# A linear attention fused with a gated feed-forward block: another table of orders, engines, PSUM banks and load places

## The chip, the cores and the metric

The kernel runs on one core of one Trainium2 chip. The metric is the device time of one execution in microseconds, lower is better; the number compared is the median over several executions. The core has five engines with an instruction queue each: PE (matmul), DVE (elementwise), ACT (activations and copies), POOL (elementwise, and the issue of DMAs whose descriptors are made by software) and SP (here only DMA issues). An instruction waits in its engine's queue until what it reads is there and what it overwrites is no longer needed, and nothing behind it on that engine starts before it.

## What is computed

Inputs r, k, v, w have the shape (batch 4, heads 8, time 768, 48), u is (8, 48), and the four weights are w1 and w2 (384 x 1024), w3 (1024 x 1024) and w_out (1024 x 384), all float32. The output is 3072 x 384.

```python
def _attn_ref(r, k, v, w, u):
    state = zeros(B, H, D, D)
    for t in range(S):
        kt, vt, rt, wt = (k[:, :, t], v[:, :, t], r[:, :, t], w[:, :, t])
        cur = einsum('bhd,bhe->bhde', u[None] * kt, vt)
        y[:, :, t] = einsum('bhd,bhde->bhe', rt, state + cur)
        state = wt[:, :, :, None] * state + einsum('bhd,bhe->bhde', kt, vt)
    return y

def _moe_ref(x, w1, w2, w3, w_out):
    a = x @ w1
    b = x @ w2
    h = a * b @ w3
    return h @ w_out
```

x is y with the heads side by side, one row for each time step of each batch element.

## The kernel before

Time is cut into 6 chunks of 128 steps, and the work into 13 units, numbered 0 to 12: units 0, 1 and 2 are chunk 0 of batch element 0, of 1, and of 2 and 3; from unit 3 on each unit is one chunk of two batch elements. A unit's steps carry its number.

Within a unit the recurrence becomes matmuls over a chunk: ln (L408, ACT) takes the logarithm of w; cs (L424, PE) sums it up along time, csT (L453) does so transposed; ne, e and et (ACT) are the exponentials of these sums; KRk, KRr and KRw (DVE or POOL) scale k and r with them; trk, trr and trw (PE) transpose, trke and trre copy the transposed tiles out of PSUM. From unit 7 or 8 on, DMA transposes on SP (dtr, dtk) do this work. m (L551, PE) multiplies the scaled k and r; its result is masked to the past either by one DVE product (msk, L570), or by a copy on ACT (mcp, L557) and a mask on POOL or DVE (maff). yi (L596) and ys (L586) sum up the output on PE, from within the chunk and from the state. rk, ruk, dg and dv form the part with u, yb (L614, DVE) adds it, yt and xT (or the DMA transposes dty) make the transposed x. kv, T, S and Sb carry the state to the next chunk.

For the feed-forward block, w3 @ w_out is formed once: for each of 8 row blocks, wt (L371) transposes a block of w3, w3Te copies it out, wm (L380) multiplies it by w_out, w34e copies the product to w34. Then, for each unit and each group g of columns, a (L714) and b (L714) multiply x by w1 and w2, asb (L719, ACT) copies a out, abT (L724, DVE) multiplies it by b; o (L730) multiplies by w34, osb (L735) copies out, st (L740, SP) stores. Units 0 and 1 have half the columns of the others. The last of w3's transposes free the tile w3_bf, whose space then takes r and k of later units; wo_bf does so for v. `warm` is a run of matmuls of zeros, that touch no data.

Loads: w, k, r and v of each unit (win, kin, rin, vin) and the weights in pieces (w1, w2 in two halves, w3 in four quarters, w_out as one). Unit 0 has r, k, v and u loaded on SP as float32 and cast by rc, kc, vc, uc; all other loads of the opening are issued by POOL.

Nothing orders the work at run time but the engines' queues. The order is one written list, `ORDER`: each entry is a step and the engine that it goes to, and the kernel records the steps in that order, so that each engine's queue is the list cut down to its own entries. `BANKS` gives every step its PSUM banks (eight) and, for copies, its buffer number; a bank must be emptied by the copy of its last user before a matmul may write it. `POOL_MASK` names the m blocks that are masked by mcp and maff.

```python
for e in ORDER.split():
    name, _, eng = e.partition("@")
    if name.startswith("warm"):
        warm(int(name[4:]), int(eng))
        continue
    steps[name](eng)
```

Of the kernel before, what the change touches and what calls it, by code (L numbers as in the profile page):

```python
# [40 lines left out]
tk0=0 m0_0=4,5 M0_0=0 y0=3,4 yt0=6 kv0=6 a0_0=6 b0_0=6 sa0_0=2 a0_1=2 b0_1=0 sa0_1=0 o0_0=0 so0_0=0 cs1=7 ct1=2 tr1=0
tk1=4 m1_0=4,5 M1_0=3 y1=3,4 yt1=1 kv1=3 a1_0=1 b1_0=0 sa1_0=0 a1_1=5 b1_1=2 sa1_1=2 o1_0=1 so1_0=1 cs2=2,3 ct2=0,1
tr2=2 tk2=7 m2_0=5,6 M2_0=2 m2_1=2,3 M2_1=1 y2=4,5 yt2=1 kv2=7 a2_0=5 b2_0=4 sa2_0=1 a2_1=7 b2_1=7 sa2_1=0 a2_2=1
b2_2=4 sa2_2=0 a2_3=0 b2_3=1 sa2_3=1 o2_0=5 so2_0=3 o2_1=2 so2_1=2 cs3=5,6 ct3=5,6 tr3=4 tk3=2 m3_0=3,4 M3_0=2
m3_1=5,6 M3_1=0 y3=0,1 yt3=6 kv3=1 a3_0=5 b3_0=4 sa3_0=2 a3_1=5 b3_1=3 sa3_1=2 a3_2=2 b3_2=3 sa3_2=1 a3_3=5 b3_3=2
sa3_3=0 o3_0=2 so3_0=3 o3_1=5 so3_1=2 cs4=3,4 tr4=6 tk4=3 m4_0=4,5 M4_0=3 m4_1=2,3 M4_1=1 y4=6,7 yt4=6 kv4=4 a4_0=7
b4_0=3 sa4_0=0 a4_1=3 b4_1=4 sa4_1=0 a4_2=5 b4_2=2 sa4_2=1 a4_3=4 b4_3=6 sa4_3=2 o4_0=3 so4_0=2 o4_1=0 so4_1=3 cs5=0,1
tr5=0 tk5=4 m5_0=0,1 M5_0=3 m5_1=0,1 M5_1=2 y5=6,7 yt5=3 kv5=7 a5_0=1 b5_0=2 sa5_0=1 a5_1=4 b5_1=3 sa5_1=0 a5_2=0
b5_2=6 sa5_2=1 a5_3=5 b5_3=6 sa5_3=2 o5_0=4 so5_0=1 o5_1=3 so5_1=0 cs6=0,1 ct6=0,1 tr6=1 tk6=7 m6_0=2,3 M6_0=1
m6_1=2,3 M6_1=0 y6=0,1 yt6=7 kv6=4 a6_0=1 b6_0=0 sa6_0=2 a6_1=2 b6_1=5 sa6_1=2 a6_2=0 b6_2=7 sa6_2=1 a6_3=2 b6_3=4  # L50
sa6_3=0 o6_0=2 so6_0=1 o6_1=6 so6_1=3 cs7=6,7 tk7=0 m7_0=1,2 M7_0=2 m7_1=4,5 M7_1=3 y7=0,1 yt7=1 kv7=7 a7_0=3 b7_0=7
sa7_0=1 a7_1=4 b7_1=2 sa7_1=1 a7_2=3 b7_2=7 sa7_2=0 a7_3=6 b7_3=4 sa7_3=2 o7_0=2 so7_0=2 o7_1=4 so7_1=0 cs8=1,2
m8_0=5,6 M8_0=0 m8_1=2,3 M8_1=1 y8=0,1 kv8=6 a8_0=5 b8_0=6 sa8_0=0 a8_1=3 b8_1=3 sa8_1=1 a8_2=6 b8_2=5 sa8_2=0 a8_3=7
b8_3=5 sa8_3=2 o8_0=7 so8_0=1 o8_1=2 so8_1=1 cs9=4,5 m9_0=4,5 M9_0=3 m9_1=0,1 M9_1=2 y9=0,1 kv9=7 a9_0=0 b9_0=3
sa9_0=1 a9_1=1 b9_1=6 sa9_1=0 a9_2=4 b9_2=7 sa9_2=2 a9_3=4 b9_3=2 sa9_3=2 o9_0=7 so9_0=2 o9_1=6 so9_1=0 cs10=5,6
m10_0=2,3 M10_0=0 m10_1=0,1 M10_1=1 y10=6,7 kv10=4,5 a10_0=4 b10_0=3 sa10_0=2 a10_1=4 b10_1=5 sa10_1=2 a10_2=4 b10_2=5
sa10_2=1 a10_3=2 b10_3=2 sa10_3=0 o10_0=3 so10_0=3 o10_1=5 so10_1=2 cs11=0,1 m11_0=4,5 M11_0=2 m11_1=6,7 M11_1=3
y11=0,1 a11_0=2 b11_0=4 sa11_0=1 a11_1=1 b11_1=7 sa11_1=0 a11_2=6 b11_2=4 sa11_2=0 a11_3=0 b11_3=6 sa11_3=2 o11_0=7
so11_0=0 o11_1=2 so11_1=0 cs12=0,1 m12_0=2,3 M12_0=1 m12_1=4,5 M12_1=0 y12=0,1 a12_0=2 b12_0=1 sa12_0=0 a12_1=7
# [6 lines left out]
m_0_0@PE w3_0@POOL u@SP uc@ACT mask@POOL rin_1@POOL vin_0@SP vc_0@ACT kv_0@PE ruk_0@DVE dg_0@DVE dv_0@POOL csT_2@PE
ne_2@ACT KRk_2@DVE trk_2@PE trw_2@PE S_0@DVE msk_0_0@DVE yi_0_0@PE kin_1@POOL rk_2@DVE et_2@ACT trke_2@ACT w1_1@POOL
ruk_2@POOL KRw_2@DVE yb_0@DVE warm5@3 m_2_0@PE m_2_1@PE mcp_2_1@ACT ln_1@ACT msk_2_0@DVE warm4@6 cs_1@PE yi_2_0@PE
dg_2@DVE csT_1@PE pc_1@ACT ne_1@ACT wt_0_0@PE wt_0_1@PE maff_2_1@DVE yt_0@PE xT_0@ACT yi_2_1@PE pc_2@ACT kv_2@PE
et_1@ACT dv_2@DVE KRk_1@DVE wt_1_0@PE trw_1@PE wt_1_1@PE yb_2@DVE yt_2@PE a_0_1@PE KRw_1@DVE trk_1@PE xT_2@ACT  # L70
trke_1@ACT a_2_3@PE S_2@DVE m_1_0@PE w3Te_1@ACT a_2_2@PE w1_0@POOL a_0_0@PE a_2_1@PE w2_1@POOL asb_2_2@ACT vin_1@POOL
b_2_3@PE w3Te_0@DVE msk_1_0@DVE rk_1@POOL yi_1_0@PE a_2_0@PE ruk_1@DVE dg_1@DVE dv_1@DVE Sb_2@DVE asb_2_3@ACT
abT_2_3@DVE yb_1@DVE b_0_1@PE yt_1@PE xT_1@DVE asb_0_0@ACT asb_2_0@ACT kv_1@PE b_2_2@PE abT_2_2@DVE a_1_0@PE
asb_0_1@ACT abT_0_1@DVE w2_0@POOL b_0_0@PE a_1_1@PE b_2_0@PE asb_2_1@ACT S_1@DVE b_1_1@PE wo@POOL abT_0_0@DVE wm_1@PE
asb_1_1@ACT b_2_1@PE w34e_1@DVE abT_2_1@DVE win_3@POOL ln_3@ACT wm_0@PE cs_3@PE ne_3@ACT b_1_0@PE w3_1@POOL wt_2_0@PE
wt_2_1@PE csT_3@PE asb_1_0@ACT abT_1_1@DVE Sb_0@DVE wt_3_0@PE abT_2_0@DVE kin_3@POOL KRk_3@DVE wt_3_1@PE w3Te_2@DVE
rin_3@POOL trk_3@PE rk_3@DVE trw_3@PE w34e_0@ACT wm_2@PE pc_3@ACT et_3@ACT KRw_3@DVE trke_3@ACT m_3_1@PE w34e_2@DVE
m_3_0@PE w3_2@POOL wt_4_0@PE wt_4_1@PE win_4@POOL w3Te_3@ACT wm_3@PE wt_5_0@PE wt_5_1@PE msk_3_1@DVE mcp_3_0@ACT
maff_3_0@DVE w3Te_4@ACT wm_4@PE abT_1_0@DVE w3_3@POOL w34e_3@DVE ln_4@ACT Sb_1@ACT iw_4@ACT vin_3@POOL w3Te_5@DVE
cs_4@PE ruk_3@DVE e_4@ACT dg_3@DVE w34e_4@DVE ys_3@PE ne_4@ACT wt_6_0@PE wt_6_1@PE w3Te_6@DVE wm_5@PE wt_7_0@PE  # L80
wt_7_1@PE yi_3_0@PE yi_3_1@PE dv_3@DVE yb_3@DVE win_5@POOL ln_5@ACT w3Te_7@DVE rin_4@POOL rw_4@DVE wm_6@PE w34e_6@ACT
cs_5@PE pc_5@ACT yt_3@PE xT_3@DVE ne_5@ACT pc_4@ACT wm_7@PE a_3_1@PE KRr_4@DVE trr_4@PE e_5@ACT kin_4@POOL KRk_4@DVE
trk_4@PE rk_4@DVE kv_3@PE w34e_7@DVE vin_4@POOL kv_4@PE trre_4@DVE iw_5@ACT asb_3_1@ACT w34e_5@ACT o_0_0@PE T_4@DVE
ruk_4@DVE rin_5@POOL trke_4@ACT m_4_1@PE T_3@DVE m_4_0@PE ys_4@PE rw_5@DVE msk_4_1@DVE osb_0_0@ACT win_6@POOL ln_6@ACT
dg_4@DVE o_1_0@PE osb_1_0@ACT o_2_1@PE osb_2_1@ACT st_2_1@SP cs_6@PE ne_6@ACT b_3_1@PE msk_4_0@DVE kin_5@POOL
# [704 lines left out]
```

## Time and profile before

| | us |
|---|---|
| median of 3 executions | 168.65 |
| lowest and highest of them | 168.05 and 200.98 |
| the profiled execution | 168.6 |
| its span, from the first to the last instruction | 166.9 |

The profile is one execution of the program taken by the hardware profiler. Its busy times are shares of the span; matmuls are pipelined and their ends modelled, so that a busy PE isn't PE at its peak. What a stage costs is read from the wait that ends last in it: the timeline names, in brackets, the idle time before an instruction and what ended it. Idle time of an engine that isn't the bound costs nothing. The names there are those of tiles: lw is written by ln, NEt by ne, ETt by et, KR by KRk and KRr, KRT by the transposed copies, Mbf by msk, mcp and maff, w_bf stands for all weight tiles, banks is PSUM.

### The profile page before, as it was taken

What the parts mean: (1) busy time and instruction counts of PE and PEld (TensorE: products, weight loads), DVE (VectorE), ACT (ScalarE), POOL (GpSimd) and SP (SyncE); (2) the same over time, 40 slices, a digit from 0 to 9 for tenths busy, and PEclk for the clock granted to TensorE, in tenths of its full rate; (3) what the DMA queues carried; (4) which work ended last, traced back from release to release, by engine and by line L of the source; (5) the groups of instructions that cost most, each with busy time, mean ns of one, the idle gap of its engine ahead of it and who ended that gap; (6) DMA issues with size and microseconds to landing.
All of it is one profiled execution on the core that took longest, in us unless ns stands there. A gap on an engine that the chain in (4) does not pass through costs nothing.

```text
span 166.9 us, 4592 instructions
## 1 busy us (share of the span) xinstructions
PE 154.8 (93%) x1912; PEld 118.1 (71%) x1913; DVE 129.7 (78%) x203; ACT 96.9 (58%) x160; POOL 106.7 (64%) x96
## 2 busy tenths in 40 slices
...
GB/s 113 215 163 180 163 188 195 245 168 245 207 151 180 141 65 235 144 157 240 108 180 195 147 207 157 84 96 172 187 137 97 108 164 164 20 166 116 4 113 125
DMA packets 100789, 25.63 MB, mean 154 GB/s; under 512 B 92928, under 2 KB 98688, under 8 KB 100768
## 3 DMA queue, kind: packets, MB, share of 16 engines
...
q14 instruction: 6, 0.05, 0.1%
...
## 4 chain that ended last, share of the span: by engine, by line
PE 74%; DVE 13%; DMA 5%; issue 4%; ACT 3%; POOL 1%; DVEq 0%; ACTq 0%; POOLq 0%
PE banks L714 31%; PE banks L730 16%; PE banks L380 6%; DMA win<-in_w_dram 5%; PE banks L551 4%; DVE Mbf L570 3%; PE banks L596 2%; PE banks L371 2%; PE banks L512 2%; DVE dv L539 2%; PE banks L424 2%; DVE KR L445 2%; PE banks L667 2%; PE banks L633 1%; DVE yb L614 1%
## 5 line engine op out<-in xcount | busy, mean ns | idle before, releaser
L714 PE MATMUL banks<-xT,w_bf 128*128 128x256 bf16 (+1 forms) x624 | 69.6, 264 | 1.7 <-DVE Mbf L570 1.7
L714 PEld LDWEIGHTS <-w_bf 128*128 128x128 bf16 x624 | 55.7, 98 | 9.4 <-issue 2.1
L719 ACT COPY a_sb<-banks 128x512 f32<-128x512 f32 x48 | 27.3, 590 | 25.8 <-PE banks L714 14.0
L724 DVE TENSOR_TENSOR abT<-a_sb,banks 128x512 bf16<-128x512 f32 x48 | 31.8, 681 | 8.6 <-PE banks L714 5.7
L730 PE MATMUL banks<-w,abT 128*128 128x384 bf16 x192 | 34.2, 326 | 0.0
L730 PEld LDWEIGHTS <-abT 128*128 128x128 bf16 x192 | 18.1, 98 | 10.7
L570 DVE TENSOR_TENSOR Mbf<-banks,mask 128x1024 bf16<-128x1024 f32 x14 | 17.1, 1218 | 4.3 <-PE banks L551 4.3
L735 ACT COPY osb<-banks 128x384 f32<-128x384 f32 x19 | 9.0, 480 | 14.1 <-PE banks L730 13.1
L614 DVE TENSOR_TENSOR yb<-banks,dv 128x768 bf16<-128x768 f32 (+1 forms) x13 | 11.6, 890 | 4.4 <-POOL dv L539 2.4
L335 POOL DMA_DIRECT2D win<-in_w_dram x12 | 13.9, 1158 | 1.4 <-POOLq L774 0.8
L408 ACT ACTIVATE lw<-win 128x768 bf16<-128x768 f32 (+1 forms) x13 | 10.4, 802 | 6.9 <-DMA win<-in_w_dram 6.9
L557 ACT CAST Mbf<-banks 128x1024 bf16<-128x1024 f32 x10 | 10.2, 1016 | 5.2 <-PE banks L551 3.7
L441 ACT ACTIVATE NEt<-banks 128x768 bf16<-128x768 f32 (+1 forms) x13 | 9.9, 761 | 4.2 <-PE banks L424 2.5
L565 POOL TENSOR_SCALAR_AFFINE_SELECT Mbf<-Mbf 128x1024 bf16<-128x1024 bf16 x5 | 5.4, 1102 | 10.5 <-ACT Mbf L557 10.5
L380 PE MATMUL banks<-wo_bf,w3T 128*128 128x384 bf16 x64 | 11.7, 326 | 0.0
L530 DVE TENSOR_REDUCE dg<-ruk 128x16 f32<-128x768 bf16 (+1 forms) x13 | 11.5, 885 | 0.1
L335 POOL DMA_DIRECT2D vin<-in_v_dram x8 | 9.1, 1140 | 3.8 <-DMA wo_bf<-in_moe_w_out_dram 3.2
L335 POOL DMA_DIRECT2D kin<-in_k_dram x8 | 9.1, 1142 | 3.0 <-PE banks L380 2.7
L335 POOL DMA_DIRECT2D rin<-in_r_dram x8 | 9.0, 1128 | 2.9 <-DMA w_bf<-in_moe_w_dram 2.2
L308 PE MATMUL banks<-zeros 128*128 128x512 bf16 x26 | 9.5, 525 | 1.5 <-DVE zeros L249 1.3
L486 POOL TENSOR_TENSOR KR<-rw,Et 128x768 bf16<-128x768 bf16 x3 | 4.9, 1639 | 8.5 <-DVE rw L478 5.4
L424 PE MATMUL banks<-lw,LT 128*128 128x384 bf16 x24 | 6.2, 325 | 2.7 <-ACT lw L408 1.8
(102 smaller groups left out, 257.2 us busy)
## 6 DMA issues: line engine op xcount, KB each, us to landing
out_dram<-osb SPq DMA_DIRECT2D x24, 192.0 KB, 2.3
...
w_bf<-in_moe_w_dram POOLq DMA_DIRECT2D x4, 512.0 KB, 13.3
...
kin<-in_k_dram POOLq DMA_DIRECT2D x7, 192.0 KB, 9.3
rin<-in_r_dram POOLq DMA_DIRECT2D x7, 192.0 KB, 9.5
vin<-in_v_dram POOLq DMA_DIRECT2D x7, 192.0 KB, 7.5
wo_bf<-in_moe_w_out_dram POOLq DMA_DIRECT2D x1, 768.0 KB, 10.6
```

Of the source, the lines that this page charges most:

```text
L335: QUEUE[eng].dma_start(dst, src)
L380: nc.tensor.matmul(one(f"wm{fi}")[:, :DM], lhsT=w3T[fi % 2][:, gi, :], rhs=wo_bf[:, gi, :], start=(gi == 0), stop=(gi == FI - 1))
L408: nc.scalar.activation(LW[:, :, :D], ww, Act.Ln)
L441: nc.scalar.activation(N_.rearrange("t (b h) d -> t b (h d)", b=nb), cs_view(), Act.Exp, scale=-1.0)
L530: nc.vector.reduce_sum(dgs, ruks, axis=AX.X)
L557: copier(eng)(Mbf[bank[f"M{t}_{b}"]], mview())
L570: nc.vector.tensor_mul(Mbf[bank[f"M{t}_{b}"]], mview(), mask.rearrange("s (j q) t -> s j q t", j=2))
L614: nc.vector.tensor_add(ybs.rearrange("t b (q e d) -> t e (b q) d", e=2, d=D), yview().rearrange("t e (x d) -> t e x d", d=D), dvs.rearrang ...
L714: nc.tensor.matmul(o[:, f, :], lhsT=wt[:, di, fi * P:(fi + 1) * P], rhs=x[:, di, :T], start=(di == 0), stop=(di == DI - 1))
L719: copier(eng)(a_sb[bank[f"sa{t}_{g}"]], one(f"a{t}_{g}"))
L724: nc.vector.tensor_mul(ab[:, g * per:(g + 1) * per, :T], sa.rearrange("p (f t) -> p f t", t=T), one(f"b{t}_{g}").rearrange("p (f t) -> p f ...
L730: nc.tensor.matmul(one(f"o{t}_{b}")[:, :DM], lhsT=ab[:, fi, b * C:(b + 1) * C], rhs=w34[:, fi, :], start=(fi == 0), stop=(fi == FI - 1))
```

## The change

Three tables are replaced: `POOL_MASK`, `BANKS` and `ORDER`. Functions, shapes, buffers and the arithmetic stay as they are. Every step is there before and after; the matmuls of zeros were 27, in runs of 13, 5, 3 and 6, and are 32, in runs of 17, 2, 3, 3, 4 and 3.

```diff
-POOL_MASK = {(2, 1), (3, 0), (5, 1), (6, 1), (7, 1), (8, 0), (8, 1), (10, 0), (11, 1), (12, 1)}
+POOL_MASK = {(2, 1), (5, 1), (6, 1), (7, 1), (8, 1), (9, 1), (10, 0), (11, 0), (12, 0)}
...
-wt0=3 wm0=3 wt1=6 wm1=0 wt2=7 wm2=7 wt3=1 wm3=1 wt4=2 wm4=5 wt5=7 wm5=7 wt6=6 wm6=5 wt7=2 wm7=2 cs0=0 ct0=1 tr0=7
+wt0=7 wm0=3 wt1=6 wm1=6 wt2=2 wm2=2 wt3=7 wm3=4 wt4=3 wm4=2 wt5=7 wm5=7 wt6=4 wm6=4 wt7=3 wm7=3 cs0=5 ct0=0 tr0=3
...
-table@ACT zeros@DVE padkr@DVE padet@DVE padlw@DVE win_0@POOL ln_0@ACT padr@DVE ones@DVE win_2@POOL kin_2@POOL LT@POOL
+table@ACT zeros@DVE vin_0@SP win_0@POOL kin_0@SP ones@DVE win_2@POOL kin_2@POOL rin_2@POOL padet@DVE I128@POOL u@SP
```

Steps that change their engine: osb of 1_0, 2_1, 3_1, 4_1, 5_0, 8_1 and 9_0 from ACT to DVE, of 5_1 and 10_0 from DVE to ACT; KRk of 0, 7, 9 and 11 from POOL to DVE, of 1 and 12 from DVE to POOL; S of 3, 4 and 7 to POOL, of 9 and 10 to DVE; dv of 6 and 10 to POOL, of 7 and 11 to DVE; rk of 8 and 11 to POOL, of 1 and 9 to DVE; ruk of 1 to POOL, of 2 and 9 to DVE; rw of 10 to POOL; maff of 2_1 and 7_1 from DVE to POOL; rc_0 from DVE to ACT and vc_0 from ACT to DVE; Sb, trke, xT, w3Te and w34e each in two to four cases; win_9 from SP's queue to POOL's.

The end of the list: before, the order on PE behind the last b was b_12_1, o_11_1, o_10_1, o_12_1, o_12_0, o_11_0; now it is b_12_1, o_11_1, o_11_0, o_12_0, o_12_1.

Three places in the engines' queues follow. In these rows a number behind a tile's name is its buffer, and a last number its place among all tiles.

First, ACT at the program's start, from ln_0 on, as one piece of the difference. win_0 is unit 0's w, win_2 unit 2's, win_1 unit 1's.

```order
 L408 ACTIVATE lw_0_82<-win_0_78 128x8x48
 L441 ACTIVATE NEt_0_90<-banks_61 128x384
+L330 CAST rin_0_62<-wide_r0_156 128x8x48
+L304 CAST u_bc_153<-u_f_154 128x384
 L459 ACTIVATE ETt_0_92<-banks_61 128x4x128
 L408 ACTIVATE lw_0_82<-win_2_80 128x16x48
-L436 ACTIVATE pc_0_112<-banks_61 128x4
-L304 CAST u_bc_153<-u_f_154 128x384
-L330 CAST vin_0_72<-wide_v0_157 128x384
 L441 ACTIVATE NEt_0_90<-banks_61 128x768
 L459 ACTIVATE ETt_0_92<-banks_61 128x8x128
+L436 ACTIVATE pc_0_112<-banks_61 128x4
```

The casts of r and u now stand ahead of et_0 and of unit 2's ln; the cast of v has left ACT. On SP, the four loads of unit 0 went out in the order r, k, u, v and now do in the order v, k, u, r.

Second, POOL in the opening, from w1's first half on; before:

```order
L346 DMA w1_bf_141<-in_moe_w1_dram 128x3x512
L524 TENSOR_TENSOR ruk_0_104<-rk_0_102,u_bc_153 128x768
L346 DMA w1_bf_141<-in_moe_w1_dram 128x3x512
L350 DMA w2_bf_142<-in_moe_w2_dram 128x3x512
L335 DMA vin_1_73<-in_v_dram 128x8x48
L520 TENSOR_TENSOR rk_1_103<-rin_1_63,kin_1_68 128x384
L350 DMA w2_bf_142<-in_moe_w2_dram 128x3x512
L354 DMA wo_bf_144<-in_moe_w_out_dram 128x8x384
L335 DMA win_3_81<-in_w_dram 128x16x48
L361 DMA w3_bf_143<-in_moe_w3_dram 128x2x1024
```

and now:

```order
L346 DMA w1_bf_141<-in_moe_w1_dram 128x3x512 x2
L350 DMA w2_bf_142<-in_moe_w2_dram 128x3x512
L445 TENSOR_TENSOR KR_1_95<-kin_1_68,NEt_1_91 128x8x48
L565 AFFINE_SELECT Mbf_2_100<-Mbf_2_100 128x1024
L335 DMA vin_1_73<-in_v_dram 128x8x48
L350 DMA w2_bf_142<-in_moe_w2_dram 128x3x512
L354 DMA wo_bf_144<-in_moe_w_out_dram 128x8x384
L524 TENSOR_TENSOR ruk_1_105<-rk_1_103,u_bc_153 128x384
L335 DMA win_3_81<-in_w_dram 128x16x48
L361 DMA w3_bf_143<-in_moe_w3_dram 128x2x1024
```

Both halves of w1 and the first of w2 now go out with no product between them; KRk_1, the mask of 2_1 and ruk_1 have come to POOL, ruk_2 and rk_1 have left it, and win_3 stands behind ruk_1.

Third, DVE around the m block of unit 9, before (msk_9_1, T_9, KRk_10 and msk_9_0 are the second to the fifth row):

```order
L724 TENSOR_TENSOR abT_7_136<-a_sb_1_127,banks_61 128x512
L570 TENSOR_TENSOR Mbf_2_100<-banks_61,mask_149 128x1024
L674 TENSOR_TENSOR Tst_0_116<-banks_61,Sst_0_118 128x384
L445 TENSOR_TENSOR KR_0_94<-w3_bf_143,NEt_0_90 128x16x48
L570 TENSOR_TENSOR Mbf_3_101<-banks_61,mask_149 128x1024
L724 TENSOR_TENSOR abT_7_136<-a_sb_0_126,banks_61 128x512
```

and now (rk_9, an abT, KRk_10, msk_9_0, ruk_9 and dg_9):

```order
L520 TENSOR_TENSOR rk_1_103<-w3_bf_143 128x768
L724 TENSOR_TENSOR abT_7_136<-a_sb_2_128,banks_61 128x512
L445 TENSOR_TENSOR KR_0_94<-w3_bf_143,NEt_0_90 128x16x48
L570 TENSOR_TENSOR Mbf_0_98<-banks_61,mask_149 128x1024
L524 TENSOR_TENSOR ruk_1_105<-rk_1_103,u_bc_153 128x768
L530 TENSOR_REDUCE dg_1_107<-ruk_1_105 128x16
```

Block 1 of unit 9 is no longer masked there (it goes by ACT and POOL), T_9 has moved to later, rk_9 and ruk_9 have come from POOL, and msk_9_0 still follows KRk_10.

172 lines of the change are left out of this document (86 added, 86 removed).

## The prediction

> **What bounds the kernel now.** I read the page's busy times first, then PE by stages, then the chain of waits, then the opening instruction by instruction. Lines of the page: busy time, share of the span, instructions.
>
> ```profile
> PE 154.8 (93%) x1912; PEld 118.1 (71%) x1913; DVE 129.7 (78%) x203; ACT 96.9 (58%) x160; POOL 106.7 (64%) x96
> ```
>
> The same by stages: in each row the stretch, its length, then busy time of PE, PEld, DVE, ACT, POOL.
>
> ```profile
> 20.00:36.00 16.00, 14.79 (x225) 13.02 (x221) 12.01 (x21) 8.14 (x16) 12.11 (x13) 1.00 1.41 201
> 36.00:60.00 24.00, 24.00 (x330) 17.83 (x328) 21.25 (x36) 17.13 (x28) 12.18 (x11) 1.00 1.95 176
> 60.00:84.00 24.00, 23.28 (x347) 18.84 (x345) 22.87 (x32) 18.44 (x31) 22.10 (x19) 1.00 1.96 165
> 84.00:96.00 12.00, 11.45 (x143) 9.10 (x141) 11.17 (x19) 9.30 (x15) 9.32 (x7) 1.00 1.71 176
> 96.00:115.00 19.00, 17.89 (x240) 13.75 (x238) 18.49 (x24) 13.64 (x23) 15.96 (x12) 1.00 1.31 140
> 115.00:164.00 49.00, 48.18 (x533) 37.62 (x530) 31.26 (x47) 21.55 (x38) 17.62 (x14) 1.00 0.72 122
> ```
>
> From 36 us on PE is the bound: its idle time there is 0, 0.72, 0.55 and 1.11 us, and after 115 nothing until its last matmul. So a new order has three places to gain: the opening up to 36 us, 2.4 us of idle PE in the middle, and the tail. DVE is a close second: from 36 to 115 us it is busy 73.8 of 79 us, so 5.2 us are free. The chain of waits, in order of time, gives the joints:
>
> ```profile
> 23.39 0.51 PE banks L633 x6
> ...
> 34.91 1.30 PE banks L380 x8
> ...
> 47.66 0.55 PE banks L371 x8
> ...
> 143.59 5.90 PE banks L714 x54
> ...
> 156.68 6.51 PE banks L730 x40
> 163.26 0.48 ACT osb L735
> ```
>
> 23.39 is yt_2, the transpose that lets unit 2 into the wide matmuls; 34.91 is wm_1, the first product of w3 and w_out; 163.26 is the last copy. 54 matmuls in 5.90 us make 0.109 us each for 256 columns, 8 transposes in 0.45 to 0.55 us some 0.056 each.
>
> **The opening, step by step.** These are timeline rows of before: start, duration, what.
>
> ```profile
> 1.25 5.73 PE L308 MATMUL banks<-zeros 128*128 128x512 bf16 x13 [1.25 <-DVE zeros L249]
> 2.77 0.43 SPq L326 DMA_DIRECT2D wide_v<-in_v_dram  x1
> 7.50 0.32 PE L424 MATMUL banks<-lw,LT 128*128 128x384 bf16 x1 [0.52 <-ACT lw L408]
> 8.25 0.59 ACT L459 ACTIVATE ETt<-banks 128x512 bf16<-128x512 f32 x1
> 10.33 0.84 ACT L408 ACTIVATE lw<-win 128x768 bf16<-128x768 f32 x1 [1.49 <-DMA win<-in_w_dram]
> 11.14 0.50 ACT L304 CAST u_bc<-u_f 128x384 bf16<-128x384 f32 x1
> 11.23 0.48 PE L424 MATMUL banks<-lw,LT 128*128 128x384 bf16 x2 [1.31 <-ACT lw L408]
> 11.54 0.51 ACT L330 CAST vin<-wide_v 128x384 bf16<-128x384 f32 x1
> 11.95 0.81 ACT L441 ACTIVATE NEt<-banks 128x768 bf16<-128x768 f32 x1
> 12.79 1.22 DVE L445 TENSOR_TENSOR KR<-kin,NEt 128x768 bf16<-128x768 bf16 x1 [0.18 <-ACT NEt L441]
> 13.00 1.02 ACT L459 ACTIVATE ETt<-banks 128x1024 bf16<-128x1024 f32 x1 [0.24 <-PE banks L453]
> 15.14 1.01 ACT L516 COPY KRT<-banks 128x1024 bf16<-128x1024 bf16 x1 [1.12 <-PE banks L512]
> 17.49 0.62 PE L551 MATMUL banks<-KRT 64*128 64x128 bf16 x16
> 17.93 1.23 DVE L570 TENSOR_TENSOR Mbf<-banks,mask 128x1024 bf16<-128x1024 f32 x1 [0.70 <-PE banks L551]
> 19.07 0.94 DVE L530 TENSOR_REDUCE dg<-ruk 128x16 f32<-128x768 bf16 x1
> 19.93 0.68 DVE L563 TENSOR_TENSOR Mbf<-Mbf,mask 128x1024 bf16<-128x1024 bf16 x1
> 20.52 1.67 DVE L539 TENSOR_TENSOR dv<-vin,dg 128x768 bf16<-128x768 bf16 x1
> 22.39 0.94 DVE L614 TENSOR_TENSOR yb<-banks,dv 128x768 bf16<-128x768 f32 x1
> 23.05 1.17 POOL L335 DMA_DIRECT2D win<-in_w_dram  x1
> ```
>
> And issue to landing (last figure, us) of SP's fourth load, and of the last w3 load, issued at 29.07:
>
> ```profile
> wide_v<-in_v_dram SPq DMA_DIRECT2D x1, 192.0 KB, 7.2
> ...
> w_bf<-in_moe_w_dram POOLq DMA_DIRECT2D x1, 512.0 KB, 16.1
> ```
>
> SP's queue. r of unit 0 changes places with v: it was the first load there; as fourth it lands where v did, 2.77 + 7.2 = 9.97. ACT now has rc_0 and uc ahead of et_0 and ln_2, so they queue behind that landing: rc_0 9.97 to 10.48 (0.51, the equal cast of v), uc to 10.98, et_0 to 11.57, ln_2 to 12.41. cs_2 thus starts near 12.45, where it was 11.23: 1.2 us lost. Four more matmuls of zeros put cs_0 at 7.9 to 8.6 for 7.50 (13 took 5.73, 0.44 each; at full clock half); that costs nothing, since et_0 waits for 10.98 anyway. If r came early, it would cost up to 1.1.
>
> What makes it up. ACT: ne_2 from 12.9 to 13.7, et_2 to 14.8, pc_0, ln_1 (half of 0.84, and a start) and pc_2 to 15.6. DVE: msk_0_0 ends at 13.9 (1.23 after dg_0), KRk_2 at 14.5 or 15.1 (half of, or all of, the 1.22 seen beside POOL's dv_0). trke_2 then ends at 16.6 to 17.3, m_2_1 follows, and msk_2_0 starts at 17.6 to 18.4, behind yb_0, rk_2, S_0 and ruk_2 on DVE: before 17.93. Behind it DVE has lost maff_2_1 (0.68), which goes to POOL: dg_2 ends 2.15 after msk_2_0's start, dv_2 takes 0.95 (like dg_2) to 1.67, yb_2 0.94. yt_2 so starts between 21.7 and 23.3, and was at 23.39. I take the middle, 22.5, as neither end of the two unknown contentions is nearer: 0.9 us won, bounds 0.1 and 1.7.
>
> From yt_2 to wm_1 before took 11.52 us. In it lie 126 matmuls of L714, 42 with 256 columns (4.6 us) and 84 with 128 (half of 0.109 each, 4.6), and 13 transposes, m_1_0, yi_1_0 and kv_1 with 1.4: 10.6 in all, so 0.9 is waiting. Now trk_1 (0.2) is done ahead of yt_2, where PE waits, and b_0_1 (0.65) stands between yi_1_0 and yt_1, which cover the wait for yb_1. I take 0.2 + 0.7; bounds 0.2 + 0 and 0.2 + 0.9. Opening: 0.9 + 0.9 = 1.8 won, bounds 0.3 and 2.8.
>
> Can the weights follow? w1_0 and w2_1 were issued behind ruk_2 and now come ahead of KRk_1, so they land sooner. But win_3, w3_1 and all later loads stand behind ruk_1, a POOL product that waits for rk_1, which stands behind msk_1_0 on DVE. The last w3 load landed at 29.07 + 16.1 = 45.2, its first user is at 47.66: 2.4 us of slack, more than the 1.8. Cost 0 while that cover holds.
>
> **The middle.** Here the engines change: osb goes to DVE seven times and leaves it twice, four maff leave DVE, msk gains one, KRk gains two net (three full ones in, among them units 9 and 11 from w3's space). Their groups (count, then busy, mean ns):
>
> ```profile
> L735 DVE COPY osb<-banks 128x384 f32<-128x384 f32 x5 | 2.7, 549 | 1.8 <-PE banks L730 1.8
> L563 DVE TENSOR_TENSOR Mbf<-Mbf,mask 128x1024 bf16<-128x1024 bf16 x5 | 3.4, 684 | 0.4 <-ACT Mbf L557 0.4
> L445 DVE TENSOR_TENSOR KR<-w_bf,NEt 128x768 bf16<-128x768 bf16 x2 | 3.2, 1582 | 0.0
> L570 DVE TENSOR_TENSOR Mbf<-banks,mask 128x1024 bf16<-128x1024 f32 x14 | 17.1, 1218 | 4.3 <-PE banks L551 4.3
> ```
>
> +5 x 0.549 - 4 x 0.684 + 1.218 + 2 x 0.6 to 2 x 1.58 = 2.4 to 4.4 us more on DVE; the smaller moves (w3Te, w34e, xT, rw, ruk, S) take back about 1, an estimate from their like-sized rows. So DVE carries 1.5 to 3.5 us more. It has 5.2 free from 36 to 115 us, less 1.8 if PE comes earlier: 3.4. The load just fits, with nothing to spare. For PE's 2.4 us of waits the bounds are 0 (all go) and 2.4 plus what does not fit, 1.5 to 2. I take no change: the longest wait, at 113.4, stood behind msk_9_0 and KRk_10 on DVE, and msk_9_0 still follows KRk_10. win_9 goes from SP to POOL, one more issue there; POOL is off the path at 64%, cost 0, or about one issue (1.2) if POOL holds a product up.
>
> **The tail.** Before, five o blocks (40 matmuls, 6.51) follow the last b; now four do, the fifth comes earlier. The same matmuls, one copy and one store close both. abT_12_1 is covered by the two o blocks of unit 11 (2.6 against 0.7). Change 0; bounds -0.2 and +0.7.
>
> **Sum.** The profiled execution took 168.6 us around its span of 166.9, and the median is 168.65, so one base serves: 168.6 - 1.8 + 0 + 0 = 166.8.
>
> **The clock.** Rows by stage in the opening, granted clock third from the end:
>
> ```profile
> 14.00:15.00 1.00, 0.93 (x9) 0.94 (x10) 1.00 (x3) 0.02 (x1) 1.00 (x2) 0.55 1.21 217
> 15.00:16.00 1.00, 1.00 (x15) 1.00 (x14) 0.87 (x2) 0.86 (x1) 0.27 (x2) 0.50 1.45 176
> ```
>
> The clock fell to 0.50 near 14 us, after a stretch with little matmul work, and the transposes there took twice as long. In the sum the fall stays. The new order has three matmuls of zeros between trw_0 and m_0_0 in just that stretch. [...]
>
> **The rivals.**
> - The clock stays up in the opening: the 16 transposes of trw_2 and trk_2 save 0.056 each, 0.9 us: 165.9. [...]
> - The middle's waits go too, if what PE waited for now has other matmuls ahead of it: 2.4 us more, 164.4, and with the opening's upper end (1.0 more) 163.4. For it: DVE's waits, 5.2 us, are there to be filled. Against it: DVE carries more.
> - DVE becomes the bound and gives the opening back: 3.5 us more load against 3.4 free, and contention as in the 1582 ns row: 168.6, no change. It decides if DVE is busy over 76 of the 79 us.
> - The other side: the fourth SP load governs the opening. If dv_2 and KRk_2 are both slow and win_3 behind ruk_1 is late by its 3 us (23.05 before, after rk_1 near 26 now, an estimate from the walk above), the w3 loads land at 48.2 for 45.2, past the 47.66 at which they were used: wt_7 waits, 0.6 us plus the lost 0.3 or so: 169.5, and up to 172.5 if the next loads queue behind it. It decides once w3's last load lands after 47.7.
> - The change does not do what it says: traced landings belong to the old order, and another order has others. Then gains and losses cancel: 168.6.
>
> **How the numbers follow.** Forecast (own range 165.8 to 168.3) 0.40; the clock 0.08; the middle's waits go 0.24; DVE gives it back 0.12; late loads 0.11; landings do not hold 0.05. Two per cent, about what a measurement here tells from no change, are 165.3 and 172.0. Faster by more than that: the third case, and the parts of the first two beyond their near ends, 0.32. Slower: the far part of late loads and some of DVE's, 0.10. Within: 0.58. The range takes the waits' far end, 163.4, and late loads to about 170.0.
>
> **What would show it.** Right: cs_2 near 12.4, yt_2 at 22.5, wm_0 near 33.8, wt_7_0 without a DMA wait, PE idle of 2 to 3 us from 36 to 115, end 10.2 after the last b. Wrong: rc_0 long before 9.9, yt_2 after 23.4, a wait of PE for w_bf, or PE idle over 4 us with DVE full.

## The result, and the profile after

| | before | changed |
|---|---|---|
| median of 20 executions each, us | 168.37 | 169.38 |
| lowest and highest | 166.93 and 200.98 | 168.10 and 171.00 |
| ratio, 95% interval | | 1.0067 [1.0043, 1.0092] |
| the profiled execution, and its span | 168.6, 166.9 | 169.86, 168.1 |

The changed kernel is 0.7% slower (0.4 to 0.9%), where 1.8 us less were forecast. The time lies within the range, the direction was wrong. The ratio leaves out slow executions such as the one of 200.98 us, which the medians above contain. The opening did get shorter, by more than was forecast; the middle took that back, and some more. The profile after, busy time, share and instructions of each engine:

```profile
PE 156.5 (93%) x1916; PEld 118.0 (70%) x1918; DVE 131.5 (78%) x206; ACT 94.1 (56%) x154; POOL 108.5 (65%) x99
```

By stages, in the same columns as before (stretch, length, then PE, PEld, DVE, ACT, POOL, and the granted clock third from the end):

```profile
14.00:15.00 1.00, 1.00 (x22) 0.88 (x20) 0.56 (x2) 1.00 (x4) 1.00 (x2) 1.00 1.80 171
15.00:16.00 1.00, 0.89 (x7) 0.29 (x3) 1.00 (x3) 1.00 (x4) 0.53 (x1) 1.00 2.58 145
20.00:36.00 16.00, 15.58 (x196) 12.76 (x193) 11.07 (x20) 7.42 (x14) 11.46 (x13) 1.00 1.51 204
36.00:60.00 24.00, 23.91 (x347) 17.86 (x345) 21.52 (x33) 17.18 (x30) 17.15 (x15) 1.00 2.17 184
60.00:84.00 24.00, 23.49 (x336) 18.97 (x334) 23.49 (x36) 19.43 (x32) 23.37 (x21) 1.00 1.78 166
84.00:96.00 12.00, 11.36 (x162) 8.83 (x160) 11.57 (x17) 7.26 (x12) 9.15 (x9) 1.00 1.68 166
96.00:115.00 19.00, 16.37 (x217) 12.21 (x215) 16.87 (x24) 9.78 (x17) 10.82 (x8) 0.91 1.10 125
36.00:115.00 79.00, 75.12 (x1053) 57.87 (x1051) 73.46 (x106) 53.65 (x87) 60.49 (x50) 0.98 1.72 162
102.57:105.98 3.41, 3.41 (x44) 2.37 (x42) 2.64 (x6) 1.96 (x3) 1.85 (x2) 0.50 1.43 221
```

Two things are to be seen. From 20 to 36 us PE's idle time fell from 1.21 to 0.42 us. And from 96 to 115 us it rose from 1.11 to 2.63 us, and there the mean clock is 0.91: the clock was at half from 102.6 to 106.0, 3.41 us. The same fall of 3.41 us that before had in the opening, at 14.1, isn't in the opening any more (rows 14 to 16: 1.00).

The joints of the chain of waits of the changed kernel (start, duration, what), to be set beside those of before:

```profile
101.77 0.51 PE banks L633 x6
102.28 2.16 PE banks L714 x12
...
158.75 5.21 PE banks L730 x32
163.99 0.48 ACT osb L735
```

101.77 is yt_7, the transposes of unit 7's output. The 12 matmuls behind it took 2.16 us, 0.18 each, where the prediction's row of before has 0.109. PE stood ahead of yt_7 for the longest time after the start, as the list of PE's waits says (engine, line, who was waited for: us in total, times, longest):

```profile
PE banks L633 <- DVE yb L614: 2.9, 2, 2.6
```

So the account of the two profiled executions reads like this. The first product of the w3 block starts at 32.77 us (wm_0) where it started at 34.75 (wm_1; the chain above names 34.91, since it counts from the end of the matmul before): 2.0 us won; the first o block starts at 53.59 for 55.92: 2.3 us won, and o_5_1 at 97.68 for 99.95 still has 2.3 (PE has the same steps ahead of these two places in both kernels, but for the matmuls of zeros and one exchanged group, b_6_0 for a_6_3). From 36 to 115 us PE idles 79 - 75.12 = 3.9 us for 79 - 76.61 = 2.4 (the four rows of before added up): 1.5 us lost. In the 3.41 us at half clock PE was busy throughout, so up to 1.7 us are lost; an experiment below puts it at 1.5, of which only some 0.9 would have been saved without the fall, as is said there. That leaves -2.3 + 1.5 + 1.5 = +0.7, and the last copy starts at 163.99 for 163.26: +0.7. From that copy's start to the end of the span it takes 168.1 - 163.99 = 4.1 us for 166.9 - 163.26 = 3.6: +0.5. The sum is 1.2, the difference of the spans.

Why yb_7 was late is seen on DVE and POOL. DVE in the changed kernel (start, duration, line, operation, output and inputs):

```profile
90.34 0.68 DVE L724 TENSOR_TENSOR abT<-a_sb,banks 128x512 bf16<-128x512 f32 x1
90.93 3.00 DVE L478 TENSOR_TENSOR rw<-w_bf,iw 128x768 bf16<-128x768 bf16 x1
93.86 0.55 DVE L445 TENSOR_TENSOR KR<-w_bf,NEt 128x768 bf16<-128x768 bf16 x1
94.33 0.55 DVE L735 COPY osb<-banks 128x384 f32<-128x384 f32 x1
94.80 1.27 DVE L724 TENSOR_TENSOR abT<-a_sb,banks 128x512 bf16<-128x512 f32 x2
95.99 1.76 DVE L486 TENSOR_TENSOR KR<-rw,Et 128x768 bf16<-128x768 bf16 x1
97.68 0.94 DVE L530 TENSOR_REDUCE dg<-ruk 128x16 f32<-128x768 bf16 x1
98.65 1.63 DVE L539 TENSOR_TENSOR dv<-vin,dg 128x768 bf16<-128x768 bf16 x1
100.76 0.96 DVE L614 TENSOR_TENSOR yb<-banks,dv 128x768 bf16<-128x768 f32 x1 [0.47 <-DVE dv L539]
```

POOL beside it, in the same kernel:

```profile
90.63 1.22 POOL L335 DMA_DIRECT2D w_bf<-in_k_dram  x1
91.86 1.65 POOL L520 TENSOR_TENSOR rk<-w_bf 128x768 bf16<-128x768 bf16 x1
...
95.81 0.84 POOL L689 TENSOR_TENSOR Sst<-Tst,pc 128x384 f32<-128x384 f32 x1
96.59 1.20 POOL L335 DMA_DIRECT2D wo_bf<-in_v_dram  x1
97.81 1.65 POOL L478 TENSOR_TENSOR rw<-w_bf,iw 128x768 bf16<-128x768 bf16 x1
99.40 2.21 POOL L539 TENSOR_TENSOR dv<-wo_bf,dg 128x768 bf16<-128x768 bf16 x1
```

And rw_9 on DVE and dv_7 on POOL in the kernel before, the first with POOL issuing a load beside it:

```profile
90.23 0.55 DVE L478 TENSOR_TENSOR rw<-w_bf,iw 128x768 bf16<-128x768 bf16 x1
...
91.75 1.87 POOL L539 TENSOR_TENSOR dv<-vin,dg 128x768 bf16<-128x768 bf16 x1
```

The same rw_9 takes 3.00 us instead of 0.55, and it ends at 93.93, 0.42 us after POOL's rk_10 has ended (93.51). KRr_9 takes 1.76 for 0.54. dv_7, which was on POOL, has come to DVE, right ahead of yb_7, and takes 1.63 there, where dv_2 alone takes 0.96; it ends 0.82 after POOL's rw_10. KRk_9, osb_4_1 and dg_7 now also stand ahead of yb_7. Two things thus make yb_7 late: four more steps ahead of it, whose own times are 0.55 + 0.55 + 0.94 + 0.96 = 3.0 us, and what is added by holding, 2.45 at rw_9, 1.2 at KRr_9 and 0.7 at dv_7, 4.3 us. So yb_7 starts at 100.76, where o_5_1 on PE was done at 99.1. What is held on DVE here are products whose inputs both lie in SBUF; in the same stretch abT, osb and the reduction keep their 0.67 to 0.68, 0.55 and 0.94 us, the reduction beside POOL's rw_10.

### The profile page after: what moved, and what is told of

It is laid out like the page before. It is cut to its first block, busy times and chain, and to the rows that moved or that the text cites. A ratio compares the mean times of both kernels' runs of the same rounds, so it can differ in the third digit from the quotient of the medians.

```text
span 168.1 us, 4594 instructions
## 1 busy us (share of the span) xinstructions
PE 156.5 (93%) x1916; PEld 118.0 (70%) x1918; DVE 131.5 (78%) x206; ACT 94.1 (56%) x154; POOL 108.5 (65%) x99
## 4 chain that ended last, share of the span: by engine, by line
PE 66%; DVE 11%; DMA 10%; ACT 4%; issue 2%; POOL 2%; SPq 1%; DVEq 0%
PE banks L714 26%; PE banks L730 17%; DMA rin<-in_r_dram 6%; PE banks L380 5%; DMA wide_r<-in_r_dram 4%; PE banks L551 4%; PE banks L596 3%; DVE rw L478 2%; PE banks L371 2%; PE banks L667 2%; PE banks L424 2%; PE banks L586 2%; DVE abT L724 1%; PE banks L512 1%; DVE yb L614 1%
## 5 line engine op out<-in xcount | busy, mean ns | idle before, releaser
L719 ACT COPY a_sb<-banks 128x512 f32<-128x512 f32 x48 | 28.0, 594 | 36.9 <-PE banks L714 29.6
L570 DVE TENSOR_TENSOR Mbf<-banks,mask 128x1024 bf16<-128x1024 f32 x15 | 18.1, 1218 | 1.9 <-PE banks L551 1.8
L565 POOL TENSOR_SCALAR_AFFINE_SELECT Mbf<-Mbf 128x1024 bf16<-128x1024 bf16 x8 | 8.9, 1115 | 15.7 <-ACT Mbf L557 15.6
L335 POOL DMA_DIRECT2D win<-in_w_dram x13 | 15.0, 1155 | 1.2 <-POOLq L774 0.8
L557 ACT CAST Mbf<-banks 128x1024 bf16<-128x1024 f32 x9 | 9.1, 1012 | 5.9 <-PE banks L551 5.2
L308 PE MATMUL banks<-zeros 128*128 128x512 bf16 x30 | 10.6, 492 | 1.4 <-DVE zeros L249 1.3
L735 ACT COPY osb<-banks 128x384 f32<-128x384 f32 x14 | 6.6, 480 | 7.5 <-PE banks L730 6.6
L551 PE MATMUL banks<-KRT 64*128 64x128 bf16 x192 | 8.2, 224 | 0.3 <-DVE KRT L470 0.3
L380 PEld LDWEIGHTS <-w3T 128*128 128x128 bf16 x64 | 5.8, 97 | 3.4
```

Of the source, the lines that this page charges most:

```text
L308: nc.tensor.matmul(banks[:, at, :], lhsT=zeros[:, :C], rhs=zeros, start=True, stop=True)
L335: QUEUE[eng].dma_start(dst, src)
L380: nc.tensor.matmul(one(f"wm{fi}")[:, :DM], lhsT=w3T[fi % 2][:, gi, :], rhs=wo_bf[:, gi, :], start=(gi == 0), stop=(gi == FI - 1))
L551: nc.tensor.matmul(o[:, e, q, :], lhsT=KRTs[a:a + PAD, 0, b * HP + q, :], rhs=KRTs[a:a + PAD, 1, b * HP + q, :], start=True, stop=True)
L570: nc.vector.tensor_mul(Mbf[bank[f"M{t}_{b}"]], mview(), mask.rearrange("s (j q) t -> s j q t", j=2))
L719: copier(eng)(a_sb[bank[f"sa{t}_{g}"]], one(f"a{t}_{g}"))
```

## The experiments

All of them compute the whole output. Ratios are to the kernel before, run on the same chip beside it. Starts of steps differ by up to 1 us between the profiles even where PE's order is the same (o_4_1 at 87.86 to 88.80 us in four kernels with the new opening), so that yb_7 is told beside o_4_1 below, which starts at 88.40 in the changed kernel. The theory was: the opening's gain is real and holds; it is lost in the new middle, where DVE products and POOL products of SBUF tiles hold each other up, yb_7 comes late, PE waits and its clock falls. The rivals: the gain is given back by DVE's load in any order; the gain isn't real because the landings change; the wait matters little and the clock alone does it.

**The new opening with the old middle.** The changed kernel's list up to kv_4, from there the list, engines and banks of before; for the masks each half keeps its own engine.

```diff
-POOL_MASK = {(2, 1), (5, 1), (6, 1), (7, 1), (8, 1), (9, 1), (10, 0), (11, 0), (12, 0)}
+POOL_MASK = {(2, 1), (5, 1), (6, 1), (7, 1), (8, 0), (8, 1), (10, 0), (11, 1), (12, 1)}
...
 vin_4@POOL kv_4@PE
-trre_4@DVE o_0_0@PE rin_5@POOL trke_4@ACT
+e_5@ACT rk_4@DVE trre_4@DVE asb_3_1@ACT
```

> The new order up to kv_4 (about 53 us), the old order, engines and banks from there on. Theory (the opening's gain of 2.3 us is real, and what the new kernel loses it loses in its own middle): PE is 2.3 us ahead at o_0_0, keeps most of it through the old middle, and the run is near 166.2 (165.4 to 167.0). Rival (the old middle is bound by DVE and gives any lead back): 168.4, as the kernel before.

Measured: 166.04 us, ratio 0.9846 [0.982, 0.9872], so 2.2 to 3.0 us less than before, as the theory had it. No fall of the clock. The old middle runs as it did, shifted by 2.8 us, down to its own long wait: KRk_10 takes 2.62 us again, and msk_9_0 stands behind it. The opening's gain is real, the middle of before keeps it, and DVE doesn't give it back, though from 36 to 115 us it is busy 73.55 us there, as in the changed kernel (73.46) and in before (73.78).

**The old opening with the new middle.** The other half of the pair: the list of before up to xT_3, then the changed kernel's.

```diff
-POOL_MASK = {(2, 1), (5, 1), (6, 1), (7, 1), (8, 1), (9, 1), (10, 0), (11, 0), (12, 0)}
+POOL_MASK = {(2, 1), (3, 0), (5, 1), (6, 1), (7, 1), (8, 1), (9, 1), (10, 0), (11, 0), (12, 0)}
...
-vin_0@SP win_0@POOL kin_0@SP
+padkr@DVE padet@DVE padlw@DVE win_0@POOL ln_0@ACT
```

> The old order up to xT_3 (about 53 us), the new order, engines and banks from there on. Theory (the parts add): 2.3 us more than the changed kernel, ratio near 1.02 (1.015 to 1.026), with the long wait before yt_7 and the clock fall in it. Rival (the new middle is bound by DVE from its own start, so a later start of PE only fills the wait): 1.007.

Measured: 172.37 us, ratio 1.0245 [1.0177, 1.0314]: the new middle and tail cost 3.0 to 5.3 us by themselves. The two halves multiplied give 0.9846 x 1.0245 = 1.0087, and the whole change is 1.0067, so they add up within their intervals. rw_9 takes 2.90 and KRk_9 1.98 us on DVE here too. Two things differ from what was expected. PE's long wait, 2.16 us, lies ahead of cs_10 and ends with osb_4_1, which stands on DVE behind KRk_9; yt_7 has none. And in the profiled execution the fall in the opening lasted 6.83 us (12.00 to 18.83), twice that of before, so that a part of the 3.0 to 5.3 us may be the opening's.

**Unit 7's steps back on their engines.** In the changed kernel dv_7 and KRk_9 go to POOL again, osb_4_1 to ACT, and dg_7 to its early place.

```diff
 rw_9@DVE
-KRk_9@DVE
-osb_4_1@DVE
...
 KRr_9@DVE
-dg_7@DVE
-dv_7@DVE
 yb_7@DVE
...
 maff_7_1@POOL
+dv_7@POOL
 kin_11@POOL
+KRk_9@POOL
 rk_10@POOL
...
 dg_8@DVE
+dg_7@DVE
...
 e_9@ACT
+osb_4_1@ACT
```

> The changed kernel with the four steps that load DVE ahead of yb_7 put back as they were: dv_7 and KRk_9 on POOL, osb_4_1 on ACT, dg_7 early on DVE. Theory (yb_7 is late because DVE carries these steps): yb_7 starts 2 to 2.7 us earlier, the wait at yt_7 falls under 0.5 us, no clock fall behind it, and the run is 3 to 4 us shorter, 165.5 to 166.5. Rival (POOL, with 3.2 us more, becomes late instead): 169.4 or more, and a wait of PE for POOL's rk_10 or dv_8.

Measured: 167.14 us, ratio 0.990 [0.9867, 0.9933]. yb_7 starts at 98.10 with o_4_1 at 88.80, so 3.1 us sooner after it; PE's wait ahead of yt_7 is gone, the clock stays up. These four steps are worth 1.0067 - 0.990, some 2.8 us, less than expected: the collision moved to KRr_9. DVE and POOL in this kernel:

```profile
92.19 1.50 DVE L478 TENSOR_TENSOR rw<-w_bf,iw 128x768 bf16<-128x768 bf16 x1
...
94.81 3.36 DVE L486 TENSOR_TENSOR KR<-rw,Et 128x768 bf16<-128x768 bf16 x1
```

```profile
94.45 1.66 POOL L445 TENSOR_TENSOR KR<-w_bf,NEt 128x768 bf16<-128x768 bf16 x1
96.06 1.64 POOL L520 TENSOR_TENSOR rk<-w_bf 128x768 bf16<-128x768 bf16 x1
```

KRr_9 (L486) is held through two POOL products in a row, and ends at 98.17, 0.47 us after the second.

**One product from POOL to DVE.** In the changed kernel rk_10 alone leaves POOL and stands on DVE ahead of ruk_10: DVE gets more work, and POOL only issues loads beside rw_9.

```diff
 kin_11@POOL
-rk_10@POOL
 win_12@POOL
...
 yb_7@DVE
+rk_10@DVE
 ruk_10@DVE
```

> The changed kernel with rk_10 moved from POOL to DVE, just ahead of ruk_10, that is behind yb_7. Theory (rw_9 takes 3.0 us on DVE instead of 0.55 because POOL runs rk_10 and a load issue beside it): rw_9 takes 0.6 to 1.4 us, yb_7 starts 1.6 to 2.4 us earlier, and the run is 2 to 3.5 us shorter, near 166.5. Rival (rw_9 is slow for another reason, its tile in w3's space or a DMA): rw_9 stays near 3.0 and the time at 169.4 or 0.3 above.

Measured: 167.79 us, ratio 0.9942 [0.992, 0.9964], 1.2% better than the change, some 2.1 us, at the low end of what was expected. DVE in this kernel:

```profile
90.48 0.55 DVE L478 TENSOR_TENSOR rw<-w_bf,iw 128x768 bf16<-128x768 bf16 x1
90.95 1.18 DVE L445 TENSOR_TENSOR KR<-w_bf,NEt 128x768 bf16<-128x768 bf16 x1
...
98.63 0.96 DVE L614 TENSOR_TENSOR yb<-banks,dv 128x768 bf16<-128x768 f32 x1 [0.47 <-DVE dv L539]
```

rw_9 is back at 0.55 us, and yb_7 comes 2.1 us sooner (1.7 by o_4_1, 87.94), with one product more on DVE. That product stands behind yb_7, so the steps ahead of yb_7 are the same as in the changed kernel, and what POOL does beside them is worth 1.7 us. This says nothing against the other part, the four steps that came ahead of yb_7: the run before took them away together with their collisions.

**The same product, one place later on POOL.** No engine's work changes; the load of w for unit 12 stands ahead of rk_10.

```diff
 kin_11@POOL
+win_12@POOL
 rk_10@POOL
-win_12@POOL
 vin_10@POOL
```

> The changed kernel with one place moved: on POOL the load of w for unit 12 now stands ahead of rk_10, not behind it. Every engine keeps exactly its work. Theory (a DVE product of SBUF tiles is held while POOL runs such a product beside it): rw_9 on DVE, 3.00 us in the changed kernel, goes back to 0.55, because POOL issues loads beside it; rk_10 then meets KRk_9 or KRr_9 instead and holds that one by 1 to 2 us; yb_7 comes 1 to 2 us sooner (98.5 to 99.8 for 100.76), PE's wait ahead of yt_7 falls from 2.6 to 1 to 2 us, and the clock stays up: ratio to the kernel before 0.992 to 1.000. Rival (DVE has simply too much work): yb_7 stays within 0.4 us of 100.76, the wait stays, and the ratio stays at 1.007.

Measured: 168.74 us, ratio 1.0006 [0.9985, 1.0026], just past the end of the theory's range; rw_9 and yb_7 came out otherwise than it said. DVE in this kernel:

```profile
90.92 1.95 DVE L478 TENSOR_TENSOR rw<-w_bf,iw 128x768 bf16<-128x768 bf16 x1
92.79 3.11 DVE L445 TENSOR_TENSOR KR<-w_bf,NEt 128x768 bf16<-128x768 bf16 x1
```

POOL beside it:

```profile
90.62 1.22 POOL L335 DMA_DIRECT2D w_bf<-in_k_dram  x1
91.83 1.16 POOL L335 DMA_DIRECT2D win<-in_w_dram  x1
93.00 1.66 POOL L520 TENSOR_TENSOR rk<-w_bf 128x768 bf16<-128x768 bf16 x1
94.59 1.19 POOL L335 DMA_DIRECT2D wo_bf<-in_v_dram  x1
```

rw_9 didn't go back to 0.55: it took 1.95 us although POOL was only issuing loads, and KRk_9 took 3.11 across rk_10 and the issue behind it. yb_7 came at 100.80, as in the changed kernel. So DVE products are held beside issued loads too, and the theory that only products on POOL do it falls; the same two issues at the same distance (0.3 us) left rw_9 at 0.55 in the run above. What decides between the two isn't settled. The rival that yb_7 stays late is borne out in this run, but not its reason, since the run above, with more work on DVE, was in time. PE's waits were split here (2.1 us ahead of cs_10, behind osb_4_1, and 1.2 ahead of yt_7), and the clock stayed up in the profiled execution. That gives a price for the fall: yt_7 starts at 101.82 for 101.77 in the changed kernel, and b_7_3 at 109.30 for 110.14, 0.9 us sooner after it. By the ratios the whole run is 1.0 us shorter than the changed kernel; most of its other executions show a mean clock of 0.984 to 0.99, so this isn't the fall alone.

**Both reliefs together.** Unit 7's four steps as above, and rk_10 on DVE.

```diff
 KRk_9@POOL
-rk_10@POOL
 win_12@POOL
...
 yb_7@DVE
+rk_10@DVE
 ruk_10@DVE
```

> The changed kernel with both reliefs: unit 7's four steps on their old engines and places, and rk_10 on DVE. Theory (collisions add up): KRr_9, which took 3.36 us in the first of the two beside KRk_9 and rk_10 on POOL, loses the part that rk_10 held, some 1.6 us, rk_10 itself costs DVE 0.6; yt_7 has no wait already, so PE gains only what the waits ahead of m_8_1 (abT, 1.0 us) and yi give back: ratio 0.983 to 0.990. It would still be 0.5 to 1.5 us behind the kernel with the new opening and the old middle (0.985 and, with msk_9_0 first, 0.980). Rival (the new middle is as good as the old once yb_7 comes in time): 0.980 or less. Rival (the two reliefs do the same thing twice): 0.990 to 0.994.

Measured: 165.64 us, ratio 0.9835 [0.9793, 0.9876], as the theory had it, though the interval just reaches the first rival's 0.980. KRr_9 takes 1.77, and yb_7 starts at 95.68, 5.1 us before that of the changed kernel (4.6 by o_4_1, 87.86). With five steps given other places, the change is 2.8 us faster than before (2.1 to 3.5).

**Zeros against the fall of the clock.** 12 matmuls of zeros ahead of yt_7, so that PE isn't idle there; first in PSUM bank 0, then in bank 4.

```diff
+warm0@12
 yt_7@PE
```

> The changed kernel with 12 matmuls of zeros on PE between o_5_1 and yt_7, where PE waits 2.6 us. Theory (the idle stretch makes the clock fall to half for 3.4 us behind it, a second loss beside the wait): yt_7 starts at 101.8 as before, the clock stays at 1.00 between 102 and 106, and the run is 1.3 to 1.7 us shorter, near 167.9. Rival (the slow stretch costs nothing, because DVE is late there anyway): 169.4, no change.

Measured: 171.07 us, ratio 1.0138 [1.0097, 1.018], a miss: the bank was taken, so that the zeros themselves waited for yb_7 and then stood between it and yt_7. In the profiled execution, of 172.83 us, the clock fell all the same, from 102.1 to 105.5. Four of the other five executions (170.16 to 171.09 us) have a mean clock of 0.997 or more, where a fall of 3.41 us takes off 0.010; so the loss is there without a fall too. The list of waits of the profiled execution:

```profile
PE banks L308 <- DVE yb L614: 2.6, 1, 2.6
```

```diff
+warm4@12
 yt_7@PE
```

> As the run with 12 matmuls of zeros before yt_7, but these go to bank 4, whose last reader is done by then, where bank 0 made them wait for yb_7 itself. Theory (the clock falls because PE stands idle): the zeros run from 99 to 101.6, yt_7 starts at 101.8 as in the changed kernel, the clock stays at 1.00, and the run is 1.3 to 1.7 us shorter than the changed kernel's ratio to the kernel before (1.007): 0.998 of the kernel before. Rival (the slow stretch costs nothing): 1.007.

Measured: 168.76 us, ratio 1.0014 [0.9983, 1.0045]. yt_7 starts at 103.08, 1.3 us later than in the changed kernel, but the clock stays up, and b_7_3 starts 6.84 us after yt_7 where it was 8.37: by this row the fall costs 1.5 us there. That is the most it can be: with yt_7 later, DVE had more time for what PE needs next, and where yt_7 came at the same time and the clock stayed up (the run with rk_10 one place later) it was 0.9. Of the whole run 0.9 us are left as a gain (1.0067 to 1.0014), since the zeros hold PE up too: they run from 100.5 to 103.1, 1.3 us past the end of yb_7. That they kept the clock up isn't shown: in this execution 2.2 us of PE's waiting lay ahead of cs_10 already, behind osb_4_1 on DVE, long before the zeros:

```profile
PE banks L424 <- DVE osb L735: 2.2, 1, 2.2
```

**Two products back on POOL in the opening.** In the changed kernel ruk_2 and rk_1 return from DVE to POOL, between the loads of the weights.

```diff
 w1_1@POOL
+ruk_2@POOL
 w1_0@POOL
...
 vin_1@POOL
+rk_1@POOL
 w2_0@POOL
```

> The changed kernel with two products of the opening back on POOL, as before the change: ruk_2 between the loads w1_1 and w1_0, rk_1 behind vin_1. Theory (the opening gained because POOL only issues loads while DVE works through unit 2, so that DVE's products run at their short times, and the weights go out sooner): dv_2 takes 1.6 instead of 0.96, w1_0 is issued near 18 instead of 14, yt_2 starts 0.6 to 1.2 us later than 21.2, and a or b waits for w1 or w2: 1.0 to 2.5 us more, ratio 1.013 to 1.022. Rival (the opening gained by the order on PE alone): yt_2 stays at 21.2 and the ratio at 1.007.

Measured: 171.00 us, ratio 1.0164 [1.0108, 1.022]. yt_2 starts at 25.05 and the first w3 product at 36.30: more than the whole gain of the opening is gone, and the clock fell in the opening again, from 12.0 to 15.4. The ratio is in the theory's range, but not by its numbers: yt_2 is 3.8 us later, where 0.6 to 1.2 were expected. In this kernel dv_2, 0.96 us in the changed kernel, is held while POOL goes on with loads, KRk_1 and a mask:

```profile
20.59 3.31 DVE L539 TENSOR_TENSOR dv<-vin,dg 128x768 bf16<-128x768 bf16 x1
```

So 2.35 of the 3.8 us are the same thing with the other sign: the change took POOL products away from beside DVE's. The rest isn't taken apart: POOL, which waits 3.48 us for rk_2 ahead of ruk_2, comes later to all that follows, rc_0 landed 0.45 us later, and the clock fell.

**A version better than both.** The first kernel, with msk_9_0 put ahead of KRk_10 on DVE, so that the mask no longer waits behind the product that is held for 2.62 us.

```diff
 T_9@DVE
+msk_9_0@DVE
 KRk_10@DVE
-msk_9_0@DVE
```

> The new opening with the old rest (ratio 0.985), and msk_9_0 moved ahead of KRk_10 on DVE. Theory (KRk_10 takes 2.6 us because POOL's dv_9 runs beside it, while msk_9_0, which reads PSUM, keeps its 1.2; b_7_3 waits 1.1 us for the bank that msk_9_0 empties): msk_9_0 ends near 109.5 instead of 111.8, PE's wait at b_7_3 vanishes, ratio 0.978 (164.9 for 168.4). Rival (DVE is bound there anyway, the wait only moves to yi_9 or kv_10): 0.985.

Measured: 165.15 us, ratio 0.9801 [0.9762, 0.984], the lowest of all; the rival's 0.985 lies just outside. DVE in this kernel:

```profile
108.03 1.22 DVE L570 TENSOR_TENSOR Mbf<-banks,mask 128x1024 bf16<-128x1024 f32 x1
109.17 1.36 DVE L445 TENSOR_TENSOR KR<-w_bf,NEt 128x768 bf16<-128x768 bf16 x1
```

The mask is 2.6 us sooner, and PE's wait of 1.1 us behind it is gone; b_7_3 starts at 110.56 for 111.86, and the next wait, 0.34 us, is one for a DMA transpose.

## Why the prediction was right or wrong

- **SP's queue and cs_2.** Right: rc_0 at 10.00, cs_2 at 12.26 (forecast 12.45). With two products back on POOL the load landed 0.45 us later.
- **Opening up to yt_2: 0.9 us, bounds 0.1 and 1.7.** Mis-sized: 23.39 to 21.21, 2.2 us, beyond the upper bound. Both open durations came out at their low ends (KRk_2 0.56, dv_2 0.96), which is where 21.7 stood, and the fall of the clock that the sum kept didn't happen there: trw_2 and trk_2 took 0.61 and 0.62 us instead of 1.06 and 1.03, which is the 0.9 of the first rival. "Neither end is nearer" was the mistake: dv_2 and KRk_2 had POOL products beside them in before, and only issued loads after the change.
- **From yt_2 to the first w3 product: 0.9 us.** Wrong: 11.56 us (21.21 to 32.77) for 11.36 (23.39 to 34.75). There was no waiting to win: PE is idle for 0.21 us in this stretch of before and for 0.14 in that of the changed kernel. The 0.9 came from subtracting estimated matmul times, which were too short, from a stretch that was 0.16 too long; and b_0_1 stood between yi_1_0 and yt_1 in before too. The 0.8 us by which PE's idle time from 20 to 36 us fell lie ahead of yt_2 and are in the term above. The opening as a whole gave 2.0 to 2.3 us in the trace, and 2.6 by the run that isolates it; forecast was 1.8.
- **Weights follow in time, cost 0.** Right: PE has no wait for w_bf. The last w3 load went out 2.2 us later, at 31.28 for 29.07, and landed 0.7 us sooner, 13.2 us after its issue for 16.1. The rival of late loads, at 169.5 the nearest of all in time, didn't come; that its number is near is chance.
- **The middle, no change.** This is the step that failed. The prediction took PE's 2.4 us of waits as given, asked only whether the longest of them, behind msk_9_0 and KRk_10, would stay, and priced DVE by a sum: load against free time. The old long wait did go, and a new one of 2.6 us arose ahead of yt_7, with a fall of the clock behind it: PE's idle time rose from 2.4 to 3.9 us, and up to 1.5 more went to the half clock. The run with the old opening puts the new middle and tail at 3.0 to 5.3 us, where 0 was forecast. The load itself was forecast well, DVE is busy 1.8 us longer over the whole span (131.5 for 129.7; 1.5 to 3.5 were said); what failed is the step from a sum to a wait. From 36 to 115 us the sum is 73.46 us for 73.78 and shows nothing. Three things that the order did show were not put together: dg_7 and dv_7 had come to stand directly ahead of yb_7, KRk_9 and osb_4_1 too, and POOL had got rk_10 and rw_10 beside DVE's rw_9 and dv_7. The row that told the price stood in the prediction: KR from w_bf, 1582 ns in the mean of two, one of 0.55 and one of 2.62.
- **The rival "DVE gives the opening back" (168.6).** Near in time, but not by its mechanism: its condition was DVE busy over 76 of 79 us, and DVE was busy 73.5, and 73.2 to 74.8 in the five kernels that were faster than before.
- **"Landings do not hold".** Refuted by the new opening with the old middle.
- **The tail, 0, bounds -0.2 and +0.7.** 0.5 more from the last copy to the end. The copy is the same 0.48 and the last store lands 1.85 us after its issue in both; the 0.5 lies behind that landing, where SP's closing instructions wait longer. Within the bounds, not explained. The sign "end 10.2 after the last b" forgot the block that had moved ahead: four blocks would have made 8.9, and it was 9.4.
- **The clock.** The sum kept the fall in the opening; in the changed kernel's profile there is none there, and one in the middle. Both falls lasted 3.41 us, and in these two traces each change of the clock lies whole steps of 3.413 us behind the first entry of full clock (in before 7.27, then 14.10 and 17.51, 2 and 3 steps; in the changed kernel 7.00, then 102.57 and 105.98, 28 and 29 steps). The step that ended at 102.57 had 2.6 us of idle PE, and that ahead of the fall in before 1.7; no other step of the two traces up to the last o block has more than 1.2. That the three matmuls of zeros between trw_0 and m_0_0 keep the clock up is not shown. In the opening the clock stayed up in the profiles of all kernels with the new order but the one with ruk_2 and rk_1 back on POOL, which has the same matmuls of zeros; so these alone don't do it. Of the 20 executions of the changed kernel five show a mean clock of 0.996 or more, too high for such a fall: they took 168.10 to 170.31 us, 168.81 in the median, and the other 15 169.67. This too points to some 0.9 us for the fall; the wait ahead of it is the other part of the loss.

Of five steps of this grid the two with the most idle PE had a fall behind them, so it may count where on the grid a wait comes to lie. These are the five, with PE's busy time first behind the length: of the changed kernel and of the old opening with the new middle, both just ahead of a fall; then two of the kernel with ruk_2 and rk_1 back on POOL, and one of the kernel with rk_10 on DVE, all three without a fall behind them.

```profile
99.16:102.57 3.41, 0.80 (x11) 0.76 (x12) 2.94 (x4) 0.48 (x1) 3.41 (x3) 1.00 1.75 149
97.34:100.75 3.41, 1.25 (x25) 1.00 (x22) 3.41 (x5) 0.28 (x1) 3.40 (x4) 1.00 1.60 213
100.77:104.18 3.41, 1.96 (x13) 0.98 (x10) 3.27 (x4) 1.65 (x3) 3.39 (x3) 1.00 2.07 122
104.18:107.59 3.41, 2.18 (x35) 1.72 (x36) 3.41 (x6) 1.33 (x2) 3.39 (x3) 1.00 1.40 203
97.85:101.26 3.41, 1.62 (x18) 1.43 (x18) 2.91 (x6) 0.89 (x2) 3.39 (x3) 1.00 2.00 153
```

A wait of 2.16 us within one step was followed by a fall, a wait of 2.3 us over the border of two steps was not. PE's idle time alone doesn't settle it: the step ahead of the fall in before had 1.71 us, and the last row here, without a fall, has 1.79.

Of DVE and POOL holding each other up the rows show this: rw_9 ends 0.42 and KRr_9 0.47 us after the POOL product beside them, about such a product's own time on DVE (0.55). What reads PSUM was not held: in the traces of before and of the changed kernel 96 abT take 0.67 to 0.69 us, 15 osb 0.54 to 0.56 and 29 msk 1.21 to 1.23. Beside POOL's KRk_9 and rk_9 in before, abT_5_1 took 0.67 and yb_7 0.95 us, but ruk_8, of two SBUF tiles, 1.59. One cast of before, Sb with its single SBUF input, took 1.63 us for 0.35 beside POOL's dv_7. Two rows don't fit a DVE product that is held by a POOL product running beside it: rw_9 began 0.93 us ahead of rk_10's recorded start and still waited for it, and it took 1.95 us beside issued loads alone. Before's own trace had such a pair, KRk_10 with 2.62 us beside POOL's dv_9, and the prediction could have looked for others in the two queues; it didn't.

What stays open: why rw_9 is held beside the same load issues in one run and not in the other, what in the chip makes the two engines hold each other up, and the tail's 0.5 us.
